# The first layer of the state rows by seven quarter products, set between the products of the last batch

## The chip, the cores and the metric

The kernel runs on one core of a Trainium2 chip. The metric is the device time of one execution in microseconds, as a median of several runs. In what follows TensorE is PE (its weight loads are PEld), VectorE is DVE, ScalarE is ACT, GpSimd is POOL and SyncE, whose queue issues the DMAs, is SP.

## The reference

For each of 8 batches and 8 heads, 512 rows `x` and 32 rows `state` of width 64 attend to each other. The concatenated result is 544 rows of width 512 per batch, and these go through a two-layer network that takes the larger of two linear maps as its hidden layer.

```python
scores = scale * x @ state.T;   a  = softmax(scores);   xread = a @ state     # 512 rows per batch
scores2 = scale * state @ x.T;  a2 = softmax(scores2);  sread = a2 @ x        # 32 state rows per batch
rows = concat([xread, sread])            # (8 * 544, 512)
h1 = rows @ w1; h2 = rows @ w2           # 512 -> 1024
out = maximum(h1, h2) @ w_out            # 1024 -> 512, f32
```

## The kernel before

Since max(h1, h2) = h2 + relu(h1 - h2), the kernel keeps `wd` = w1 - w2 and folds w2 @ w_out into `wwo`. The hidden layer of some rows is then relu(rows @ wd), kept transposed with hidden units on the partitions, and the output is the hidden layer times `wo` plus rows times `wwo`.

The first batches are issued by an order written out by hand (`ORDER`). Batches 2 to 6 go through one loop (`for b in range(2, B - 1)`), which also prepares the attention of batch `n = b + 1`. Batch 7 and the 256 state rows stand in the straight code behind the loop, called the last part here. Every engine works through its own queue in the order in which the code issues.

- `l1_mm`, `l1_ev` (lines 374 and 381): the hidden layer of a batch, eight banks of two 512-column matmuls, and the relu of each bank into `r`, by ACT and DVE in turn.
- `product`, `opened`, `r_sum`, `w_sum`: the second layer. It is a 2 by 2 block product done with seven products in place of eight (Strassen's scheme, in Winograd's form). `r_sum` makes the sums of the left blocks in `st` (part of big5), four per batch on DVE; `w_sum` made those of the weights in `wt`, once, two of them on POOL. One `product` is eight 256-column matmuls. `keep` copies a partial result out of PSUM to `part` (part of big6), `put` adds it to another result into the output tile.
- `m1` (line 472): the hidden layer of the state rows, directly. Eight banks f, each four matmuls of 256 columns (`wd` as weights, `sread_t`, the transposed state rows, moving), and a relu on ACT into `rs_r` (part of w2m).
- `m_product` with `m_sum`: the second layer of the state rows, by the same seven products. `m_sum(k, aq, sst, "P")` sums blocks of `sread_t` into `sst` (xb0) on POOL at the end of the loop, `m_sum(k, bq, rst, "V")` sums blocks of `rs_r` into `rst` (sf0) on DVE.
- `mul` (line 277) is the softmax's scaling on POOL, `difference` and `v_sum` (line 404) are POOL sums of weights.
- `check_sums` (lines 676 to 678): three DVE instructions at the end of b = 6, which look for a softmax sum out of range and leave `bad`. A PE matmul (line 813) adds `bad` over the partitions. It stands in PE's queue ahead of `l1_mm` of batch 7. The general path behind the last branch isn't run here.

The PSUM banks are handed out by `bank("r")`, a ring of five.

Of the kernel before, what the change touches and what calls it, by code (L numbers as in the profile page):

```python
# [10 lines left out]
BF16 = mybir.dt.bfloat16  # L11
ACTF = mybir.ActivationFunctionType
ALU = mybir.AluOpType
# [41 lines left out]
def kernel(  # L55
# [9 lines left out]
    nc = tc.nc  # L65
    B, H, S, D = x.shape
    _, _, Ns, _ = state.shape
# [4 lines left out]
    NF = FF // 128  # L72
# [15 lines left out]
    def bank(ring="r", dtype=F32):  # L88
        if isinstance(ring, int):
            i = ring  # L90
        else:
            r = rings[ring]
            i = r[turn[ring] % len(r)]
            turn[ring] += 1
        return banks[i] if dtype == F32 else banks[i].bitcast(BF16)

    def copy(eng, o, i):
        if eng == "A":
            nc.scalar.copy(o, i)  # L99
        elif eng == "V":  # L100
            nc.vector.tensor_copy(o, i)  # L101
        else:
            nc.gpsimd.tensor_copy(o, i)  # L103
# [8 lines left out]
    wd, = many(1, "wd", [4, FF])  # L112
# [8 lines left out]
    rs_r = w2m[:, 0:NF * NT].rearrange("p (f t) -> p f t", f=NF)  # L121
# [15 lines left out]
    big = many(10, "big", [2048], F32)  # L137
# [11 lines left out]
    wt = big[3].bitcast(BF16).rearrange("p (k f n) -> p k f n", k=4, f=4)  # L149
    st = big[5].bitcast(BF16).rearrange("p (k f t) -> p k f t", k=4, f=4)  # L150
# [214 lines left out]
    def relu(o, p, eng=None):  # L365
        if eng is None:
            flip[0] ^= 1
            eng = "A" if flip[0] else "V"
        if eng == "A":
            nc.scalar.activation(out=o, in_=p, func=ACTF.Relu)  # L370
        else:
            nc.vector.tensor_scalar(o, p, scalar1=0.0, scalar2=None, op0=ALU.max)  # L372
# [8 lines left out]
    def l1_ev(p, b, f, eng=None):  # L381
        relu(r_s[b % 2][:, f, :], p, eng)
# [20 lines left out]
    def add(eng, o, i0, i1, op=ALU.add):  # L403
        (nc.gpsimd if eng == "P" else nc.vector).tensor_tensor(o, i0, i1, op=op)  # L404

    def wq(j, k):
        return wo[:, 4 * j:4 * j + 4, 256 * k:256 * k + 256]

    def rq(b, i, j):
        return r_s[b % 2][:, 4 * j:4 * j + 4, 256 * i:256 * i + 256]  # L410
# [5 lines left out]
    def r_sum(b, k, eng):  # L416
        a, c, op = ((rq(b, 1, 0), rq(b, 1, 1), ALU.add), (st[:, 0], rq(b, 0, 0), ALU.subtract),
                    (rq(b, 0, 0), rq(b, 1, 0), ALU.subtract), (rq(b, 0, 1), st[:, 1], ALU.subtract))[k]
        add(eng, st[:, k], a, c, op)
# [5 lines left out]
    def product(pv, lhs, rhs, first=False, cc=(0, 1)):  # L425
        for c in cc:
            for f in range(4):
                nc.tensor.matmul(pv[c], lhs[:, f, 128 * c:128 * c + 128], rhs[:, f, :],  # L428
                                 start=first and f == 0 and (c == 0 or pv.split), stop=False, skip_group_check=True)
# [18 lines left out]
    def keep(k, pv, eng):  # L448
        if pv.split:
            for c in range(2):  # L450
                copy(eng[c], part[:, k, 256 * c:256 * c + 256], pv[c])
        else:
            copy(eng, part[:, k], pv.p[0])
# [14 lines left out]
    def store(b, c0=0, c1=NC, lo=0, hi=DM, eng=None):  # L468
        dst = out[b * L:b * L + S].rearrange("(p c) n -> p c n", c=NC)
        (eng or nc.sync).dma_start(out=dst[:, c0:c1, lo:hi], in_=ob(b)[:, c0:c1, lo:hi])  # L470

    def m1(f, eng=None):
        p = bank("r")
        for i in range(4):
            nc.tensor.matmul(p[:, 0:NT], wd[:, i, f * 128:(f + 1) * 128], sread_t[:, i, :],  # L475
                             start=(i == 0), stop=(i == 3))
        relu(rs_r[:, f, :], p[:, 0:NT], eng)
# [14 lines left out]
    sst = xb_s[0].rearrange("p c m -> p (c m)")[:, 0:1024].rearrange("p (k f t) -> p k f t", k=4, f=2)  # L492
# [5 lines left out]
    def aq(i, j):  # L498
        return sread_t[:, 2 * j:2 * j + 2, 128 * i:128 * i + 128]
# [4 lines left out]
    def v_sum(k, eng):  # L504
        a, c = ((vq(0, 1), vq(0, 0)), (vq(1, 1), ws[:, 0]), (vq(1, 1), vq(0, 1)), (vq(1, 0), ws[:, 1]))[k]
        add(eng, ws[:, k], a, c, ALU.subtract)
# [6 lines left out]
    def m_product(p, la, lb, ra, rb, first=False):  # L513
        for f in range(2):
            nc.tensor.matmul(p, la[:, f], ra[:, f], start=first and f == 0, stop=False, skip_group_check=True)  # L515
        for f in range(4):
            nc.tensor.matmul(p, lb[:, f], rb[:, f], start=False, stop=False, skip_group_check=True)  # L517

    def m_out(t, k):
        return rs_o[:, t, 256 * k:256 * k + 256]  # L520

# [94 lines left out]
    def sw_range(b, z):  # L616
# [16 lines left out]
        wt=w_sum, rs=r_sum, dif=difference,  # L633
# [13 lines left out]
    for tok in ORDER.split():  # L647
        name, _, at_ = tok.partition("@")
        name, _, eng = name.partition(">")
# [86 lines left out]
    for b in range(2, B - 1):  # L736
        n = b + 1
        if b + 2 < B and b != 3:
            xt_dma(b + 2)
        if b < 4:  # L740
            nc.vector.reciprocal(rr_all[:, b - 2], srd[:, b - 2, 0:130:129])
        for f in range(NF):
            l1_ev(l1_mm(b, f), b, f)
        pX, pY, pZ = Pair(BX), Pair(BY), Pair(BZ)
        pp = [sc_mm(n, hh) for hh in range(2)]
        for hh in range(2):
            sc_ev(pp[hh], n, hh)
        product(pX, rq(b, 0, 0), wq(0, 0), True)
        keep(0, pX, "A")
        r_sum(b, 0, "V")  # L750
        red(n, 0)
        mul(n, 0, "P")
        r_sum(b, 1, "V")
        product(pZ, rq(b, 0, 1), wq(1, 0), True)
        opened(b, pZ, 0, so_half(b, 0))
        pg = [sw_mm(n, 512 * z, 512 * z + 512, BY if z == 0 else "r") for z in range(3)]
        sw_ev(pg[0], n, 0, 512, 0, "A")
        sw_ev(pg[0], n, 0, 512, 1, "A")
        red(n, 1)
        mul(n, 1, "P")  # L760
        at_dma(n)
        if b == 3:
            xt_dma(b + 2)
        if b == 2:
            store(1)
        if b + 4 < B - 1:
            for g in range(2):
                load_x(b + 4, g)
        elif b + 4 < B:
            load_x(b + 4, 0, n=H)  # L770
        r_sum(b, 2, "V")
        product(pX, st[:, 1], wt[:, 1])
        sw_ev(pg[1], n, 512, 1024, 0, "A")
        keep(1, pX, "A")
        put(b, 0, 0, pZ, 0)
        sw_ev(pg[1], n, 512, 1024, 1, "V")
        sw_ev(pg[2], n, 1024, 1536, 0, "A")
        product(pY, st[:, 0], wt[:, 0], True)
        keep(2, pY, "A")
        r_sum(b, 3, "V")  # L780
        sw_ev(pg[2], n, 1024, 1536, 1, "A")
        if b + 2 < B:
            for k in range(4):
                cast_e(b + 2, k, "P")
        difference(n, "P")
        if b + 3 < B:
            for g in range(2):
                cast_b(b + 3, g, "P")
        if b < 6:
            v_sum(b - 2, "P")  # L790
        product(pX, st[:, 2], wt[:, 2])
        opened(b, pX, 1, so_half(b, 1))
        p = sr_mm(n, "r")
        put(b, 1, 1, pX, 2)
        sr_ev(p, n)
        if b < 4:
            srd_ev(b - 2)
        if n == B - 1:
            check_sums()
        product(pY, st[:, 3], wq(1, 1))  # L800
        opened(b, pY, 0, so_half(b, 1))
        put(b, 0, 1, pY, 1)
        product(pX, rq(b, 1, 1), wt[:, 3])
        opened(b, pX, 1, dif[:, b % 2])
        if b < 4:
            sr_cp(sr_tr(b - 2, "r"), b - 2, "A")
        sr_cp(sr_tr(n, "r"), n, "A")
        put(b, 1, 0, pX, None, "A")
        if n == B - 1:
            for k in range(4):  # L810
                m_sum(k, aq, sst, "P")
            p = bank("r")
            nc.tensor.matmul(p[:, 0:1], full, bad, start=True, stop=True)
            nc.vector.tensor_copy(flag[0:1, :], p[0:1, 0:1])
        store(b)


    b = B - 1
    for f in range(NF):
        l1_ev(l1_mm(b, f), b, f)  # L820
    for k in (0, 1, 2, 3):
        r_sum(b, k, "V")
    for f in range(NF):
        m1(f, "A")
    fv = nc.values_load(flag[0:1, 0:1], skip_runtime_bounds_check_because="compared with zero alone")
    pX, pY, pZ = Pair(BX, "r"), Pair(BY), Pair(BZ)
    product(pX, rq(b, 0, 0), wq(0, 0), True)
    keep(0, pX, "AV")
    product(pZ, rq(b, 0, 1), wq(1, 0), True)
    opened(b, pZ, 0, so_half(b, 0))  # L830
    put(b, 0, 0, pZ, 0)
    store(b, 0, 2, 0, 256)
    for k in (0, 1, 2, 3):
        m_sum(k, bq, rst, "V")
    product(pX, st[:, 1], wt[:, 1])
    keep(1, pX, "AV")
    product(pY, st[:, 0], wt[:, 0], True)
    keep(2, pY, "A")
    tc.mark_branch_hint_location("gen", "LikelyTaken", [ENG.PE, ENG.Activation, ENG.DVE, ENG.Pool, ENG.SP])
    mX, mY, mZ = (bank("r")[:, 0:256] for _ in range(3))  # L840
    m_product(mX, aq(0, 0), bq(0, 0), vq(0, 0), wq(0, 0), True)
    copy("A", mk[:, 0], mX)
    m_product(mZ, aq(0, 1), bq(0, 1), vq(1, 0), wq(1, 0), True)
# [63 lines left out]
```

## Time and profile before

| | |
|---|---|
| time, three runs | 143.7, 144.05, 144.55 us; median 144.05 us |
| span of the profiled execution | 141.9 us; its own time isn't listed, and the median lies 2.15 us above the span |
| granted PE clock, mean | 0.995 |
| PE busy / DVE / ACT / POOL | 132.1 / 103.9 / 88.4 / 72.6 us |
| chain that ended last, by engine | PE 85%, DMA 6%, DVE 2%, SP's queue 2% |
| first layer of the state rows, `m1` | 3.49 us on the chain, from 121.93 us |

A row of the timeline has the start, the length from the first start to the last end, the engine, the line, the operation and its tiles, and in brackets the idle time ahead of it with what released it. A row of the chain has start, share of the chain in us, and what. A group has busy time, mean ns of one instruction, and idle time. A PE matmul's length in a row is longer than the step to the next matmul, because matmuls overlap.

### The profile page before, as it was taken

To read this page: it belongs to the slowest core of one execution; us is meant where nothing else is said; L and a number is where in the kernel's file an instruction comes from. 1 tells how busy PE (TensorE), PEld (TensorE's weight loads), DVE (VectorE), ACT (ScalarE), POOL (GpSimd) and SP (SyncE) were. 2 spreads that over 40 slices of the span, in tenths; PEclk is the share of its full clock that TensorE was granted. 3 is DMA by queue.
4 is the path that set the end of the run, shared out by engine and by line. 5 is a ranking of instruction groups with operands and counts; after the bars stand their busy time and mean duration, and the time that the engine had idled before them with its cause. 6 is when DMAs were issued, how large, how long until landed. Compare 5 with 4: busy or idle time off the path is not lost.

```text
span 141.9 us, 3651 instructions
## 1 busy us (share of the span) xinstructions
PE 132.1 (93%) x1432; PEld 93.6 (66%) x1442; DVE 103.9 (73%) x193; ACT 88.4 (62%) x172; POOL 72.6 (51%) x99
## 2 busy tenths in 40 slices
PE   6585999999999999999999999999999999999980
PEld 2264735456787776786778577857876786788860
DVE  3488969778999748984898489569948986848320
ACT  4367968886599547665874769087737745753220
POOL 4147326089109993599179809963980544200000
PEclk9999999999999999999999999999999999999998
DMA  4999999954999999999947999669217041502073
GB/s 120 332 372 389 388 381 388 347 100 78 180 316 288 72 273 259 248 255 270 390 167 137 222 385 161 134 222 225 48 34 296 2 79 69 229 0 79 2 257 120
DMA packets 36452, 29.50 MB, mean 208 GB/s; under 512 B 22608, under 2 KB 32336, under 8 KB 35536
## 3 DMA queue, kind: packets, MB, share of 16 engines
q1 hardware_dynamic: 36160, 29.10, 74.9%
q8 instruction: 12, 0.20, 0.6%
q10 hardware_dynamic: 272, 0.13, 0.3%
q14 instruction: 8, 0.07, 0.1%
HBM read 15.20 MB, written 8.91 MB: 170 GB/s over the span
## 4 chain that ended last, share of the span: by engine, by line
PE 85%; DMA 6%; DVE 2%; SPq 2%; ACT 1%; issue 1%; DVEq 0%
PE bank L428 36%; PE bank L377 18%; PE bank L434 10%; DMA big<-in_moe_w_dram 6%; PE bank L354 5%; PE bank L608 5%; PE bank L475 2%; PE bank L517 2%; PE bank L261 2%; PE bank L301 2%; SPq L164 1%; PE bank L515 1%; DVE w2m L101 1%; DVE r L372 1%; PE bank L550 1%
## 5 line engine op out<-in xcount | busy, mean ns | idle before, releaser
L372 DVE TENSOR_SCALAR r<-bank 128x512 bf16<-128x512 f32 x32 | 21.9, 690 | 13.0 <-PE bank L377 11.9
L277 POOL TENSOR_TENSOR a<-e,er 128x512 bf16<-128x512 bf16 x14 | 17.2, 1235 | 27.4 <-ACT big L99 16.3
L99 ACT COPY big<-bank 128x512 f32<-128x512 f32 (+2 forms) x40 | 21.9, 552 | 12.8 <-PE bank L434 5.5
L377 PE MATMUL bank<-at,sw 128*128 128x512 bf16 x120 | 29.1, 379 | 0.6 <-DVE sw L101 0.2
L428 PEld LDWEIGHTS <-big 128*128 128x128 bf16 x256 | 23.9, 98 | 6.1 <-DVE big L404 2.1
L99 ACT CAST sw<-bank 128x512 bf16<-128x512 f32 x36 | 20.1, 609 | 6.0 <-PE bank L354 6.0
L428 PE MATMUL bank<-big,big 128*128 128x256 bf16 x192 | 23.1, 273 | 0.1
L404 DVE TENSOR_TENSOR big<-bank,big 128x512 f32<-128x512 f32 (+1 forms) x25 | 16.5, 663 | 8.3 <-PE bank L434 7.9
L377 PEld LDWEIGHTS <-sw 128*128 128x128 bf16 x128 | 12.2, 97 | 13.5 <-ACT sw L99 0.5
L370 ACT ACTIVATE r<-bank 128x512 bf16<-128x512 f32 x32 | 18.3, 596 | 4.1 <-PE bank L377 3.9
L428 PEld LDWEIGHTS <-r 128*128 128x128 bf16 x192 | 18.2, 98 | 2.7 <-issue 0.5
L103 POOL CAST xe<-big 128x512 bf16<-128x512 f32 x23 | 15.6, 709 | 6.2 <-DMA big<-in_x_dram 6.2
L103 POOL CAST xb<-big 128x1024 bf16<-128x1024 f32 x12 | 13.1, 1111 | 4.7 <-DMA big<-in_x_dram 4.7
L428 PE MATMUL bank<-wo,r 128*128 128x256 bf16 x128 | 15.5, 273 | 0.0
L434 PE MATMUL bank<-sw,at 128*128 128x256 bf16 x96 | 14.4, 273 | 0.0
L99 ACT COPY sread_t<-bank 128x128 bf16<-128x128 bf16 x8 | 3.2, 472 | 17.3 <-PE bank L338 14.0
L434 PEld LDWEIGHTS <-at 128*128 128x128 bf16 x128 | 12.5, 98 | 1.7
L404 DVE TENSOR_TENSOR big<-r 128x1024 bf16<-128x1024 bf16 x16 | 11.6, 723 | 0.6
L273 DVE TENSOR_REDUCE sums<-e 128x16 f32<-128x512 bf16 x16 | 10.8, 674 | 0.0
L269 ACT ACTIVATE e<-bank 128x512 bf16<-128x512 f32 x16 | 8.9, 596 | 1.9 <-PE bank L261 1.4
L404 POOL TENSOR_TENSOR big<-sw 128x512 bf16<-128x512 bf16 x8 | 9.2, 1150 | 1.3 <-issue 1.3
L101 DVE CAST sw<-bank 128x512 bf16<-128x512 f32 x12 | 7.9, 681 | 1.0 <-PE bank L354 1.0
(100 smaller groups left out, 181.8 us busy)
## 6 DMA issues: line engine op xcount, KB each, us to landing
big<-in_x_dram SPq DMA_DIRECT2D x14, 512.0 KB, 7.8
out_dram<-big SPq DMA_DIRECT2D x7, 1024.0 KB, 6.0
big<-in_moe_w_dram SPq DMA_DIRECT2D x8, 512.0 KB, 11.5
big<-in_moe_w_out_dram SPq DMA_DIRECT2D x4, 512.0 KB, 11.0
big<-in_x_dram SPq DMA_DIRECT2D x1, 1024.0 KB, 6.9
out_dram<-big SPq DMA_DIRECT2D x4, 256.0 KB, 2.7
sf<-in_state_dram SPq DMA_DIRECT2D x1, 384.0 KB, 10.4
out_dram<-w2m SPq DMA_DIRECT2D x2, 128.0 KB, 2.4
```

Of the source, the lines that this page charges most:

```text
L99: nc.scalar.copy(o, i)
L101: nc.vector.tensor_copy(o, i)
L103: nc.gpsimd.tensor_copy(o, i)
L269: nc.scalar.activation(out=e_view(e_s[b % 2], hh).rearrange("p (g c) i n -> p g c (i n)", g=2), in_=p.rearrange("p (c g m) -> p g c m", c= ...
L273: nc.vector.tensor_reduce(es_all[:, b, hh], e_view(e_s[b % 2], hh), axis=AXX, op=ALU.add)
L277: (nc.gpsimd if eng == "P" else nc.vector).tensor_mul(e_view(a_s[b % 2], hh), e_view(e_s[b % 2], hh), er_s[b % 2][:, hh].unsqueeze(3).to_b ...
L370: nc.scalar.activation(out=o, in_=p, func=ACTF.Relu)
L372: nc.vector.tensor_scalar(o, p, scalar1=0.0, scalar2=None, op0=ALU.max)
L377: nc.tensor.matmul(p, sw_s[b % 3][:, g, f * 128:(f + 1) * 128], at_s[b % 3][:, g].rearrange("p c t -> p (c t)"), start=(g == 0), stop=(g = ...
L404: (nc.gpsimd if eng == "P" else nc.vector).tensor_tensor(o, i0, i1, op=op)
L428: nc.tensor.matmul(pv[c], lhs[:, f, 128 * c:128 * c + 128], rhs[:, f, :], start=first and f == 0 and (c == 0 or pv.split), stop=False, ski ...
L434: nc.tensor.matmul(pv[c], at_s[b % 3][:, g, 2 * i + c, :], rhs[:, g, :], start=False, stop=False, skip_group_check=True)
```

## The change

`m1` is no longer called in the last part. The first layer of the state rows becomes a 2 by 2 block product with seven `q_product`s, each of eight 128-column matmuls. The four sums of blocks of `wd` are made by `d_sum` on POOL, two in b = 5 and two in b = 6, and lie in big9 (`wdt`). Three kept results go to big0 (`qk`) by ACT. `q_out` ends a block: on DVE an addition and a relu, or for the last block a relu on ACT. The `q_product`s stand between the first products of batch 7, two of the four `r_sum`s move behind them, and all four `m_sum`s of `rst` stand behind the last `q_product`. The banks of `q_product` are used again by `m_product`.

```diff
+    wdt = big[9].bitcast(BF16).rearrange("p (k f n) -> p k f n", k=4, f=2)
+    qk = big[0][:, 0:1536].rearrange("p (k n) -> p k n", k=3)
+    def dq(j, k):
+        return wd[:, 2 * j:2 * j + 2, 512 * k:512 * k + 512]
+    def d_sum(k, eng):
+        a, c = ((dq(0, 1), dq(0, 0)), (dq(1, 1), wdt[:, 0]), (dq(1, 1), dq(0, 1)), (dq(1, 0), wdt[:, 1]))[k]
+        add(eng, wdt[:, k], a, c, ALU.subtract)
+    def q_product(p, la, rd, first=False):
+        for t in range(4):
+            for f in range(2):
+                nc.tensor.matmul(p[:, 128 * t:128 * t + 128], rd[:, f, 128 * t:128 * t + 128], la[:, f],
+                                 start=first and t == 0 and f == 0, stop=False, skip_group_check=True)
+    def q_out(i, k, p, kept=None):
+        o = rs_r[:, 4 * k:4 * k + 4, 128 * i:128 * i + 128]
+        if kept is None:
+            relu(o, p.rearrange("p (f t) -> p f t", f=4), "A")
+        else:
+            add("V", o, p.rearrange("p (f t) -> p f t", f=4), qk[:, kept].rearrange("p (f t) -> p f t", f=4))
+            nc.vector.tensor_scalar(o, o, scalar1=0.0, scalar2=None, op0=ALU.max)
...
         if b < 6:
             v_sum(b - 2, "P")
+        if b in (5, 6):
+            for k in (0, 1) if b == 5 else (2, 3):
+                d_sum(k, "P")
         product(pX, st[:, 2], wt[:, 2])
...
-    for k in (0, 1, 2, 3):
+    for k in (0, 1):
         r_sum(b, k, "V")
-    for f in range(NF):
-        m1(f, "A")
     fv = nc.values_load(flag[0:1, 0:1], skip_runtime_bounds_check_because="compared with zero alone")
     pX, pY, pZ = Pair(BX, "r"), Pair(BY), Pair(BZ)
+    qX, qY, qZ = (bank("r") for _ in range(3))
+    q_product(qX, aq(0, 0), dq(0, 0), True)
+    copy("A", qk[:, 0], qX)
+    q_product(qZ, aq(0, 1), dq(1, 0), True)
+    q_out(0, 0, qZ, 0)
     product(pX, rq(b, 0, 0), wq(0, 0), True)
     keep(0, pX, "AV")
+    q_product(qY, sst[:, 0], wdt[:, 0], True)
+    copy("A", qk[:, 2], qY)
+    q_product(qX, sst[:, 1], wdt[:, 1])
+    copy("A", qk[:, 1], qX)
     product(pZ, rq(b, 0, 1), wq(1, 0), True)
     opened(b, pZ, 0, so_half(b, 0))
     put(b, 0, 0, pZ, 0)
     store(b, 0, 2, 0, 256)
+    q_product(qX, sst[:, 2], wdt[:, 2])
+    q_out(1, 1, qX, 2)
+    q_product(qY, sst[:, 3], dq(1, 1))
+    q_out(0, 1, qY, 1)
+    for k in (2, 3):
+        r_sum(b, k, "V")
+    product(pX, st[:, 1], wt[:, 1])
+    keep(1, pX, "AV")
+    q_product(qX, aq(1, 1), wdt[:, 3])
+    q_out(1, 0, qX)
+    product(pY, st[:, 0], wt[:, 0], True)
+    keep(2, pY, "A")
     for k in (0, 1, 2, 3):
         m_sum(k, bq, rst, "V")
-    product(pX, st[:, 1], wt[:, 1])
-    keep(1, pX, "AV")
-    product(pY, st[:, 0], wt[:, 0], True)
-    keep(2, pY, "A")
...
-    mX, mY, mZ = (bank("r")[:, 0:256] for _ in range(3))
+    mX, mY, mZ = (q[:, 0:256] for q in (qX, qY, qZ))
```

POOL's queue from the end of b = 5 to the end of b = 6, before. In order: `difference`, `v_sum`, the two `mul`s of batch 7, `difference`, and the first `m_sum` into xb0.

```order
L404 TENSOR_TENSOR big6_115<-sw0_102 128x512
L404 TENSOR_TENSOR sb0_82<-wwo0_76,sb0_82 128x512
L277 TENSOR_TENSOR a1_94<-e1_92,er1_96 128x8x64 x2
L404 TENSOR_TENSOR big6_115<-sw1_103 128x512
L404 TENSOR_TENSOR xb0_89<-sread_t0_78 128x256
```

The two `mul`s follow straight on `v_sum`, and the `m_sum`s straight on `difference`. The same place in the changed kernel, where big9 holds the sums of `wd`:

```order
L404 TENSOR_TENSOR big6_115<-sw0_102 128x512
L404 TENSOR_TENSOR sb0_82<-wwo0_76,sb0_82 128x512
L404 TENSOR_TENSOR big9_118<-wd0_75 128x1024
L404 TENSOR_TENSOR big9_118<-wd0_75,big9_118 128x1024
L277 TENSOR_TENSOR a1_94<-e1_92,er1_96 128x8x64 x2
L404 TENSOR_TENSOR big6_115<-sw1_103 128x512
L404 TENSOR_TENSOR big9_118<-wd0_75 128x1024
L404 TENSOR_TENSOR big9_118<-wd0_75,big9_118 128x1024
L404 TENSOR_TENSOR xb0_89<-sread_t0_78 128x256
```

Two sums of 1024 elements came in ahead of the `mul`s of batch 7, and two behind the last `difference`, ahead of the `m_sum`s.

DVE's queue in the last part, before, from the third `r_sum` (into big5) over the load of the flag, `keep` and `put` to the first two `m_sum`s (into sf0):

```order
L404 TENSOR_TENSOR big5_114<-r1_106 128x1024
L404 TENSOR_TENSOR big5_114<-r1_106,big5_114 128x1024
L825 TENSOR_LOAD flag0_811
L101 COPY big6_115<-bank3_66 128x256
L404 TENSOR_TENSOR big7_116<-bank0_63,big6_115 128x2x256
L404 TENSOR_TENSOR sf0_81<-w2m0_80 128x512
L404 TENSOR_TENSOR sf0_81<-sf0_81,w2m0_80 128x512
```

All four `r_sum`s stand ahead of `keep` here, and the `m_sum`s straight behind `put`. The changed kernel's DVE queue from that `keep` to the same two `m_sum`s; the instructions that write w2m are those of `q_out`:

```order
L101 COPY big6_115<-bank6_69 128x256
L404 TENSOR_TENSOR big7_116<-bank0_63,big6_115 128x2x256
L404 TENSOR_TENSOR w2m0_80<-bank2_65,big0_109 128x4x128
L541 TENSOR_SCALAR w2m0_80<-w2m0_80 128x4x128
L404 TENSOR_TENSOR w2m0_80<-bank5_68,big0_109 128x4x128
L541 TENSOR_SCALAR w2m0_80<-w2m0_80 128x4x128
L404 TENSOR_TENSOR big5_114<-r1_106 128x1024
L404 TENSOR_TENSOR big5_114<-r1_106,big5_114 128x1024
L101 COPY big6_115<-bank6_69 128x256
L404 TENSOR_TENSOR sf0_81<-w2m0_80 128x512
L404 TENSOR_TENSOR sf0_81<-sf0_81,w2m0_80 128x512
```

Between `put` and the first `m_sum` there stand now two blocks of `q_out`, two `r_sum`s and the second `keep`.

## The prediction

> **What bounds the kernel now.** I read the page first, then the chain that ended last, then the timeline of each engine from 104 us on. The page gives PE as the bound:
>
> ```profile
> span 141.9 us, 3651 instructions
> PE 132.1 (93%) x1432; PEld 93.6 (66%) x1442; DVE 103.9 (73%) x193; ACT 88.4 (62%) x172; POOL 72.6 (51%) x99
> ```
>
> The chain in the last 25 us has almost nothing but PE in it:
>
> ```profile
> 118.45 0.00 PE bank L813
> 118.46 0.24 PE bank L377
> ...
> 118.75 3.18 PE bank L377 x14
> 121.93 3.49 PE bank L475 x32
> 125.42 1.75 PE bank L428 x16
> 127.17 0.44 PE bank L434 x4
> ```
>
> So a microsecond taken from PE here is a microsecond of the span, and so is each wait put into PE's queue. `m1` takes 3.49 us for 32 matmuls, 0.109 each; two products take 1.75 us. L813 is the matmul that reads `bad`; it costs nothing today because DVE is done in time.
>
> **PE's own saving.** Removed: 32 matmuls of 256 columns, 3.49 us. Added: seven products of eight 128-column matmuls, 56, each with its own weights. The nearest rows are 128-column transposes, each with its own weights, and the weight loads themselves:
>
> ```profile
> 13.51 1.07 PE L550 MATMUL bank<-ident,wb 128*128 128x128 bf16 x16 [1.35 <-ACT wb L99]
> L475 PEld LDWEIGHTS <-wd 128*128 128x128 bf16 x32 | 3.1, 98 | 0.6
> ```
>
> One such matmul alone reads 0.22 us long (its group's mean is 220 ns), so the 16 step by (1.07 - 0.22) / 15 = 0.057 us, though a load reads 98 ns: loads overlap. 56 x 0.057 = 3.17 us, so 0.32 us are saved. Bounds: half of a 256-column step (0.0545) gives 3.05 us and 0.44 saved; loads that did not overlap give 56 x 0.098 = 5.49 us and 2.0 lost. I take 0.32, by the transposes, which are the same form.
>
> **POOL's four new sums.** These, not the products, decide my forecast. What they run beside:
>
> ```profile
> 104.64 1.15 POOL L404 TENSOR_TENSOR sb<-wwo,sb 128x512 bf16<-128x512 bf16 x1
> 111.28 1.31 POOL L277 TENSOR_TENSOR a<-e,er 128x512 bf16<-128x512 bf16 x1 [5.50 <-ACT big L99]
> 115.38 1.16 POOL L404 TENSOR_TENSOR big<-sw 128x512 bf16<-128x512 bf16 x1 [1.29 <-issue]
> 119.01 0.67 POOL L404 TENSOR_TENSOR xb<-sread_t 128x256 bf16<-128x256 bf16 x1 [2.47 <-ACT sread_t L99]
> 109.51 0.69 DVE L404 TENSOR_TENSOR big<-r 128x1024 bf16<-128x1024 bf16 x1
> 111.07 0.63 DVE L404 TENSOR_TENSOR big<-big,r 128x1024 bf16<-128x1024 bf16 x1
> 112.03 1.53 PEld L428 LDWEIGHTS <-big 128*128 128x128 bf16 x15 [0.42 <-DVE big L404]
> 116.59 0.29 DVE L676 TENSOR_SCALAR wb<-sums 128x272 f32<-128x272 f32 x1
> 116.92 0.44 DVE L677 TENSOR_TENSOR wb<-wb,sums 128x272 f32<-128x272 f32 x1
> 117.40 0.44 DVE L678 TENSOR_REDUCE bad<-wb 128x1 bf16<-128x272 f32 x1
> ```
>
> POOL looks idle (5.50 us, then 2.47 us), and one would hide the sums there. But the trace shows that POOL and DVE hold each other up when both read SBUF. The price of one sum, and four meetings:
>
> ```profile
> 29.75 2.12 POOL L404 TENSOR_TENSOR big<-wo 128x1024 bf16<-128x1024 bf16 x1
> 34.89 1.15 POOL L404 TENSOR_TENSOR big<-sw 128x512 bf16<-128x512 bf16 x1
> 35.48 1.11 DVE L404 TENSOR_TENSOR big<-r 128x1024 bf16<-128x1024 bf16 x1
> 42.55 2.06 POOL L277 TENSOR_TENSOR a<-e,er 128x512 bf16<-128x512 bf16 x2 [6.52 <-DVE er L274]
> 43.70 1.45 DVE L404 TENSOR_TENSOR big<-big,r 128x1024 bf16<-128x1024 bf16 x1
> 44.55 1.07 POOL L103 CAST xe<-big 128x512 bf16<-128x512 f32 x1
> 45.08 1.09 DVE L404 TENSOR_TENSOR big<-r 128x1024 bf16<-128x1024 bf16 x1
> 8.23 0.61 POOL L103 CAST xe<-big 128x512 bf16<-128x512 f32 x1 [1.12 <-DMA big<-in_x_dram]
> 8.50 0.63 DVE L101 CAST xe<-big 128x512 bf16<-128x512 f32 x1
> ```
>
> The DVE sum takes 0.63 to 0.69 us alone. At 35.48 it ends at 36.59, 0.55 after POOL's end at 36.04; at 43.70 it ends at 45.15, 0.54 after POOL's second `mul` at 44.61; at 45.08 at 46.17, 0.55 after the cast at 45.62. DVE waits for the whole POOL instruction and then does its own reading. At 8.50 a cast with one SBUF input does the same: 9.13, 0.29 after POOL's 8.84. Where DVE comes first, POOL waits (the 1.31 us at 111.28, against 1.03 for each `mul` at 42.55). The Trainium skill says the same as a rule (SBUF — State Buffer, Who interferes with whom): the shared port pair is an exclusive lock, taken by a DVE instruction with two SBUF inputs or in a two-port mode, and the later one blocks entirely; reductions never do. By that rule L676 and L677 are both exposed and L678 is not; the meeting of a sum with L676's kind is not in this trace, only the cast's.
>
> End of b = 5. The two sums run from 105.79 (end of the 104.64 row) to 105.79 + 2 x 2.12 + 0.07 for the dependence = 110.10, ahead of the `mul` at 111.28. The DVE sum due at 109.51 waits to 110.10 and ends at 110.65 in place of 110.20, 0.45 late; so the second one (111.07) ends at 112.15, and the weights that PE loads from it at 112.03 come some 0.15 us late: **+0.15**, between 0 and 0.25. `mul` and the transposes' DMA slip by 0.45 too, covered by the stall that follows.
>
> End of b = 6. The third sum follows the `difference` of 115.38; POOL starts its next instruction some 0.04 before the end of the last, so at 116.50, 0.09 us ahead of L676 at 116.59. It holds the port to 118.62. L676 then needs 0.15, to 118.77; the fourth sum has asked since 118.69 and gets the port next, to 120.89. L677, which depends on L676, reads after it, to 121.19; L678 ends at 121.67. PE gets `bad` at 121.73, against 118.45: **+3.28 us**, on the chain, because the whole `l1_mm` of batch 7 is queued behind that matmul. Queued behind L676 on DVE are a `put`, the flag and the relus, none of which PE needs earlier. Bounds: 0 if DVE isn't held, 3.4 if each sum takes a gap more.
>
> The `m_sum`s on POOL move from 119.01 to 121.2, done by 124; the `q_product` that reads the first stands 5 us into PE's delayed work, so they cost nothing. Without the stall they would still be in time by about 1 us.
>
> **DVE in the last part.** Rows that price it:
>
> ```profile
> 122.76 0.69 DVE L404 TENSOR_TENSOR big<-r 128x1024 bf16<-128x1024 bf16 x1
> 123.49 0.69 DVE L404 TENSOR_TENSOR big<-big,r 128x1024 bf16<-128x1024 bf16 x1
> 124.10 0.68 DVE L404 TENSOR_TENSOR big<-r 128x1024 bf16<-128x1024 bf16 x1
> 124.70 0.68 DVE L404 TENSOR_TENSOR big<-r,big 128x1024 bf16<-128x1024 bf16 x1
> 127.70 0.69 DVE L404 TENSOR_TENSOR big<-bank,big 128x512 f32<-128x512 f32 x1 [0.94 <-PE bank L434]
> 128.31 0.42 DVE L404 TENSOR_TENSOR sf<-w2m 128x512 bf16<-128x512 bf16 x1
> 128.76 0.42 DVE L404 TENSOR_TENSOR sf<-sf,w2m 128x512 bf16<-128x512 bf16 x1
> 129.10 0.42 DVE L404 TENSOR_TENSOR sf<-w2m 128x512 bf16<-128x512 bf16 x1
> 130.62 0.42 PEld L517 LDWEIGHTS <-sf 128*128 128x128 bf16 x4
> ```
>
> Steps from start to start: 0.61 for a 0.69 instruction, 0.73 where the next depends on it, 0.45 and 0.34 for `m_sum`. On the clock of before, `put` starts 1.68 us earlier (four `q_product`s of 0.45 ahead of it in place of 3.49), at 126.02. Then come 0.61, twice an addition and a relu (0.73 + 0.21 each), two `r_sum`s (0.61 each), `keep` (0.34), two `m_sum`s (0.45 + 0.42): the second ends at 130.94. The relu over 512 bf16 in SBUF isn't in the trace; its ends are 0.29 (L676, 272 elements) and 0.42 us (`m_sum`, two inputs), less 0.08 to the next start; I take the lower, the same operation. PE wants these sums as weights at 130.62 - 0.32 = 130.30, so it waits 0.64 to 0.9 us: **+0.75**. Today they are ready 1.4 us early.
>
> Hidden: ACT's three copies and one relu, 0.6 us each, replace eight relus over 3.44 us; each is read two products later. The first two `q_product`s need banks whose relus end as PE arrives (0.05 us at most). The flag's load waits behind work already queued. No DMA is added; SP waits only for `put`.
>
> **Sum** on the profiled execution: 141.9 + 0.15 + 3.28 - 0.32 + 0.75 = 145.76 us span, and with the 2.15 us between span and median 147.9 us; the median and the profile differ by that constant alone.
>
> **Rivals.**
> 1. One of the two races goes the other way. If L676 is first (116.59), it ends at 116.88, the third sum at 119.0, L677 waiting since 116.92 at 119.3, L678 at 119.78: PE waits 1.39 us, sum 146.0. If L677 gets in between the two sums, 1.29 us; if only L677 is held, 1.0 us. So 145.6 to 146.0. For it speaks how small the margins are, 0.09 and about 0.1 us; against it, the timeline's order. Chance 0.28.
> 2. The sums don't hold up the check: `bad` is ready before PE asks at 118.39. That needs both L676 and L677 done ahead of the third sum, or a port that gives way for short reads, so the third sum starting after 117.2, or L677 held by less than 0.5 us. Then -0.32 + 0.75: 144.5, not slower by what counts, and 143.7 if DVE keeps up. For it: L676's kind isn't seen blocked here. Against: four meetings, one pattern. Chance 0.13.
> 3. PE comes back slow from a 3.3 us wait. At the kernel's start eight 512-column matmuls step far wider than the 14 of L377 above (3.18 / 14 = 0.227):
>
> ```profile
> 1.29 3.25 PE L577 MATMUL bank<-wz 128*128 128x512 bf16 x8 [1.29 <-DVE ones L580]
> ```
>
> Eight at 0.227 would take 1.8 us, so 1.4 us go: 149.3. The page TensorE: Matmul & The Clock Gate of the Trainium skill (The HAM clock gate) halves the clock after an idle window of about 3.4 us. The granted clock here is 0.995 on the mean, and no PE wait in the trace is nearly as long. Chance 0.05.
>
> **How the numbers follow.** My case, two sums and the check in turn, has 0.50, with 147.2 to 148.4 us as its own range (0.3 on the stall, 0.3 on DVE's backlog); rival 1 has 0.28, rival 2 0.13, rival 3 0.05, and 0.04 is left for loads that don't overlap or a gain I don't see. 147.9 is the first case's time. The range reaches down to rival 1's lower end less 0.3: 145.3 to 148.4. Half a per cent, 0.72 us, is about what a measurement of this kernel tells from no change: slower 0.85 (cases 1, 3 and mine, most of the rest), same 0.13 (rival 2), faster 0.02.
>
> **What will show it.** L700 (today's L676) reads about 2.1 us long from 116.6, L701 about 2.4 us; PE idles some 3.3 us ahead of the matmul that reads `bad`, and the chain goes through DVE and POOL there. The 56 products step by 0.057 us. PE's weight load from sf waits 0.6 to 0.9 us for DVE near the end. I am wrong if L700 to L702 read as today, or if the new sums take far from 2.12 us.

## The result and the profile after

| | before | changed |
|---|---|---|
| time, median | 144.12 us (143.7 to 144.55, 4 runs) | 149.11 us (147.59 to 149.79, 4 runs) |
| ratio, 95% interval | | 1.0335 [1.0298, 1.0373] |
| span of the profiled execution | 141.9 us | 145.8 us (its time: 147.59 us) |

The changed kernel is 3.4% slower. It was forecast slower, but the median lies 1.2 us above the predicted 147.9 us and 0.7 us outside the range. The profiled execution, 147.59 us, is the fastest of the four; the other three took 148.99 to 149.79 us, and the trace of one like those is shown under same_again.

The page of the changed kernel, the chain that ended last by engine:

```profile
PE 78%; DVE 11%; DMA 5%; ACT 2%; issue 1%; SPq 1%; POOL 1%; DVEq 0%
```

PE's share of the chain fell from 85 to 78%, and DVE's rose from 2 to 11%. Where DVE came in is seen in the timeline around the end of b = 6 (start, length, engine, line, operation, and in brackets the idle time with its releaser):

```profile
116.92 2.12 POOL L404 TENSOR_TENSOR big<-wd 128x1024 bf16<-128x1024 bf16 x1
117.07 2.12 DVE L700 TENSOR_SCALAR wb<-sums 128x272 f32<-128x272 f32 x1
118.99 2.18 POOL L404 TENSOR_TENSOR big<-wd,big 128x1024 bf16<-128x1024 bf16 x1
119.23 2.24 DVE L701 TENSOR_TENSOR wb<-wb,sums 128x272 f32<-128x272 f32 x1
121.50 0.44 DVE L702 TENSOR_REDUCE bad<-wb 128x1 bf16<-128x272 f32 x1
122.00 0.16 PE L840 MATMUL bank<-bad,full 128*128 128x1 bf16 x1 [3.07 <-DVE bad L702]
```

L700 reads 2.12 us instead of 0.29 and ends 0.15 us after the third sum (119.19 and 119.04); L701 reads 2.24 instead of 0.44 and ends 0.30 after the fourth (121.47 and 121.17). The reduction is as long as ever. PE waited 3.07 us for `bad`. The chain behind it (start, us, what):

```profile
122.45 3.18 PE bank L377 x14
125.63 0.89 PE bank L532 x16
```

In this execution PE came back at full pace: 14 matmuls of `l1_mm` in 3.18 us, as before. Two `q_product`s take 0.89 us.

### The profile page after: what moved, and what is told of

Read it like the earlier page. It is cut to its first block, busy times and chain, and to the rows that moved or that the text cites. A ratio compares the mean times of both kernels' runs of the same rounds, so it can differ in the third digit from the quotient of the medians.

```text
span 145.8 us, 3708 instructions
## 1 busy us (share of the span) xinstructions
PE 133.3 (91%) x1456; PEld 94.7 (65%) x1466; DVE 110.0 (75%) x199; ACT 87.8 (60%) x168; POOL 81.6 (56%) x103
## 4 chain that ended last, share of the span: by engine, by line
PE 78%; DVE 11%; DMA 5%; ACT 2%; issue 1%; SPq 1%; POOL 1%; DVEq 0%
PE bank L428 31%; PE bank L377 19%; PE bank L434 8%; DMA big<-in_x_dram 5%; PE bank L632 4%; PE bank L354 4%; DVE big L404 3%; PE bank L261 2%; PE bank L517 2%; PE bank L323 2%; DVE wb L701 2%; DVE wb L700 1%; PE bank L574 1%; PE bank L301 1%; PE bank L532 1%
## 5 line engine op out<-in xcount | busy, mean ns | idle before, releaser
L99 ACT COPY big<-bank 128x512 f32<-128x512 f32 (+2 forms) x43 | 23.5, 553 | 14.8 <-PE bank L434 5.5
```

## The experiments

The theory after the result had three parts: the third and fourth sum hold up the check through the port that POOL and DVE share; PE's wait of 3.07 us for `bad` follows from that; and in most executions PE then works at half its clock for a while, which is what the median has above the forecast. Rivals: the excess lies in the new products or in DVE's backlog behind them, or it is no property of the kernel.

**same_again: the changed kernel once more**, with no edit, for a trace of another execution.

> The changed kernel once more, unchanged, for a trace of one of its longer executions (the four so far: 147.6, 149.0, 149.2, 149.8 us, and the trace at hand is of the 147.6 one). Theory 1 (the check waits for GpSimd, and after that wait TensorE restarts at half its pace in most executions): in a longer execution the 16 matmuls of the hidden layer of batch 7 behind the wait take 4.5 to 5.2 us in place of 3.47, and the rest of the trace is as before. Theory 2 (the extra 1.5 us comes from somewhere else, the new products or the loads at the start): those 16 matmuls take 3.5 us, and the time is lost at another place. Median 148.5 to 149.5 us by both.

Measured: 149.77 us (148.96 to 150.4), ratio 1.0392 [1.0332, 1.0452], the traced execution 148.96 us with a span of 147.2 us. Its chain behind the wait, in which `bad` is read at 121.67:

```profile
122.12 4.87 PE bank L377 x14
126.99 0.89 PE bank L532 x16
```

The same 14 matmuls, in the same order, take 4.87 in place of 3.18 us: **+1.69 us**. Behind them both traces agree again (two `q_product`s in 0.89). PE's granted clock, asked for in windows around that place (length, PE busy with its instructions, granted clock, DMA share, GB/s), first of same_again, then of the changed kernel's first trace:

```profile
118.69:122.11 3.42, 0.40 (x2) 1.00 0.00 0
122.11:125.52 3.41, 3.40 (x8) 0.50 0.75 305
```

```profile
117.33:120.75 3.42, 1.60 (x16) 1.00 0.04 9
120.75:124.16 3.41, 2.11 (x10) 1.00 0.26 108
```

The boundaries of these windows aren't chosen freely. The trace records the clock in stretches, and their lengths are multiples of 3.413 us (39 of them between two changes in the first trace, 34 and 6 in this one), so the clock is set on a grid of 3.41 us whose place in the span is another in each execution. In same_again the idle time of PE, 118.61 to 121.67, lies almost all in one window: PE was busy for 0.40 us of it, and the next window runs at 0.50. In the first trace a boundary at 120.75 cuts the idle time in two; PE was busy for 1.60 and 2.11 us in the two windows, and the clock stays at 1.00. The page TensorE: Matmul & The Clock Gate of the Trainium skill (The HAM clock gate) says that the activity window is about 3.4 us and free-running, which these records bear out; that an idle window is needed before the clock drops is stricter than what they show, since 0.40 us of work in the window, and 1.11 us below, did not prevent it.

**fill_wait: work for PE in the wait.** Twelve dummy matmuls ahead of the one that reads `bad`, into the same bank (eleven of them are in the trace).

```diff
             p = bank("r")
+            for _ in range(12):
+                nc.tensor.matmul(p, ident, wd[:, 0, 0:512], start=True, stop=True)
             nc.tensor.matmul(p[:, 0:1], full, bad, start=True, stop=True)
```

> Twelve matmuls of 512 columns (12 x 0.217 = 2.6 us) stand ahead of the matmul that reads the check's result, in the 3.07 us in which TensorE is idle there; the wait itself stays. Theory 1 (half pace after the wait): TensorE is never idle for long, so every execution is like the short one, 147.2 to 147.9 us. Theory 2 (the extra time has another place): no help, 148.5 to 149.5 us.

Measured: 147.88 us (147.46 to 148.75), ratio 1.0255 [1.0189, 1.032]. PE's timeline:

```profile
119.05 2.54 PE L841 MATMUL bank<-wd,ident 128*128 128x512 bf16 x11
122.07 0.16 PE L842 MATMUL bank<-bad,full 128*128 128x1 bf16 x1 [0.48 <-DVE bad L702]
122.10 3.61 PE L377 MATMUL bank<-at,sw 128*128 128x512 bf16 x16
```

The stall is as long as before (`bad` comes at 122.0), only PE has something to do in it, and `l1_mm` keeps full pace. On the same chip that is 1.9 us less than same_again. So the excess over the forecast is the clock after the wait; the wait itself, the products and the backlog were all still there. (The clock is read from the one traced execution, 147.96 us; of the other three only the times are known.)

**sums_alone: the kernel before, with the four sums added** as in the change, and nobody reading them.

```diff
... (wdt, dq and d_sum as in the change)
             v_sum(b - 2, "P")
+        if b in (5, 6):
+            for k in (0, 1) if b == 5 else (2, 3):
+                d_sum(k, "P")
```

> The kernel before, with the four sums of wd added on GpSimd at the places of the changed kernel, and nothing else: their result is not used, and the first layer of the state rows is computed as before. Theory 1: the check waits for the third and fourth sum just the same, 3.3 us, and TensorE restarts slowly in most executions: 147.3 to 149.0 us. Theory 2: 147.4 us in every execution, as the extra time belongs to the products. Rival (the sums cost nothing, the loss is the products'): 144.1 us.

Measured: 149.2 us (148.89 to 150.44), ratio 1.0363 [1.0292, 1.0434]. The timeline, and PE's clock in two windows of the grid (the third and fourth sum start at 116.56 and 118.64):

```profile
116.72 2.12 DVE L686 TENSOR_SCALAR wb<-sums 128x272 f32<-128x272 f32 x1
118.87 2.24 DVE L687 TENSOR_TENSOR wb<-wb,sums 128x272 f32<-128x272 f32 x1
121.64 0.16 PE L826 MATMUL bank<-bad,full 128*128 128x1 bf16 x1 [3.07 <-DVE bad L688]
```

```profile
119.39:122.80 3.41, 1.11 (x6) 1.00 0.00 0
122.80:126.22 3.42, 3.42 (x10) 0.50 0.76 309
```

Four sums on an idle engine, in nobody's way by the program, cost 5.0 us (149.2 less 144.24); the whole change costs 5.5 on the same chip (149.77). Nearly all of the loss is the sums', not the products'.

**sums_early: the sums away from the check.** The first in b = 4, two in b = 5, the fourth on DVE behind the flag.

```diff
-        if b in (5, 6):
-            for k in (0, 1) if b == 5 else (2, 3):
+        if b in (4, 5):
+            for k in (0,) if b == 4 else (1, 2):
                 d_sum(k, "P")
...
             nc.vector.tensor_copy(flag[0:1, :], p[0:1, 0:1])
+            d_sum(3, "V")
```

> The changed kernel with its sums elsewhere: the first in b = 4, two in b = 5 on GpSimd, where it idles, and the fourth on VectorE behind the flag. The check meets no sum. Theory 1: the 3.1 us wait and the slow restart both go; what stays is 0.1 us in b = 6, -0.37 us for the products and 0.6 us for VectorE's backlog: 144.1 to 144.6 us. Theory 2: the wait goes, but 1.5 us stay: 145.6 to 146.2 us.

Measured: 145.28 us (144.72 to 146.22, 10 runs), ratio 1.0066 [1.0031, 1.0101]: most of the loss is gone, but it is 0.7 us above the range I gave. The timeline and the chain of one execution (146.0 us) say why:

```profile
109.04 2.13 POOL L404 TENSOR_TENSOR big<-wd 128x1024 bf16<-128x1024 bf16 x1
110.55 1.17 DVE L404 TENSOR_TENSOR big<-r 128x1024 bf16<-128x1024 bf16 x1
117.81 0.29 DVE L700 TENSOR_SCALAR wb<-sums 128x272 f32<-128x272 f32 x1
120.42 1.89 PE L377 MATMUL bank<-at,sw 128*128 128x512 bf16 x7 [0.76 <-DMA at<-a]
```

```profile
115.64 4.75 DMA at<-a
```

The check (L700) reads 0.29 us again. What is late is `at`. The last transposes of batch 7 were issued at 115.64, against 114.12 before: 1.04 us of this the execution had lost earlier (`l1_mm` of batch 6 starts at 106.10 instead of 105.06), and 0.48 us come from the sum at 109.04, which held up an `r_sum` (1.17 us instead of 0.69) and all that follows it on DVE. Then they took 4.75 us to land, where before took 3.1. PE waits 0.76 us for them.

**no_check: the changed kernel without the check.** The three DVE instructions are left out (`bad` is set to zero), so the sums stand where the change put them but have nothing to hold up there.

```diff
         if n == B - 1:
-            check_sums()
+            nc.vector.memset(bad, 0.0)
```

> The changed kernel with its sums where they are, but the three VectorE instructions of the check are left out (bad is set to zero; the sums' range is not looked at). Theory 1 (the loss is the check's wait for the two sums and what follows from it): TensorE's 3.1 us wait and the slow restart go; what is next is the transposes of batch 7 (at<-a), which in every kernel with these sums landed 4.7 to 4.8 us after issue, not 3.1: a wait of about 0.8 us. 145.0 to 145.6 us. Rival (the products or their banks cost the time): 147 us or more.

Measured: 145.38 us (145.26 to 146.75, 4 runs), ratio 1.0105 [1.0033, 1.0178]. The chain and the timeline:

```profile
114.64 4.75 DMA at<-a
```

```profile
119.44 1.89 PE L377 MATMUL bank<-at,sw 128*128 128x512 bf16 x7 [0.77 <-DMA at<-a]
```

Without the check 1.2 us of the loss are left (145.38 less 144.18, the kernel before on the same chip), of 5.0 us in the result and 5.5 in same_again. In the place of the wait for `bad` comes a shorter one, 0.77 us, for the same slow transposes as in sums_early. In the changed kernel they land at 119.7, inside the wait for `bad`, and so cost nothing.

**sums_placed: the sums where they hold up nobody.** The first two are cut in halves, one half in b = 4 and three in b = 5, so that POOL is done ahead of `r_sum`; the last two stand behind the check, and a copy of `bad` of one element on POOL makes them wait for it.

```diff
... (d_half is d_sum for the half f)
-        if b in (5, 6):
-            for k in (0, 1) if b == 5 else (2, 3):
-                d_sum(k, "P")
+        if b in (4, 5):
+            for k, f in ((0, 0),) if b == 4 else ((0, 1), (1, 0), (1, 1)):
+                d_half(k, f, "P")
...
             check_sums()
+            copy("P", gt, bad)
+            for k in (2, 3):
+                d_sum(k, "P")
```

> The changed kernel with its sums only where no VectorE instruction with two SBUF inputs is due: a half in b = 4, three halves in b = 5 (done by 109.2, ahead of the sum at 109.5), the last two behind the check, by a small copy on GpSimd that waits for it. Theory 1: no wait for the check, the transposes land as before; left are the products (-0.37 us) and VectorE's backlog of 0.6 us, with up to 0.4 us more for the sums beside r_sum: 144.3 to 144.9 us. Rival (the sums still hold up something): 145.3 us or more.

Measured: 144.57 us (144.27 to 145.53, 12 runs), ratio 1.0029 [0.9999, 1.006]. The timeline around the check and in the last part, and two rows of the waits from 118 us on (us in total, times, longest):

```profile
117.33 0.29 DVE L704 TENSOR_SCALAR wb<-sums 128x272 f32<-128x272 f32 x1
118.78 2.13 POOL L404 TENSOR_TENSOR big<-wd 128x1024 bf16<-128x1024 bf16 x1
119.02 0.17 PE L847 MATMUL bank<-bad,full 128*128 128x1 bf16 x1
124.22 1.04 DVE L404 TENSOR_TENSOR big<-big,r 128x1024 bf16<-128x1024 bf16 x1
125.90 0.67 DVE L545 TENSOR_SCALAR w2m<-w2m 128x512 bf16<-128x512 bf16 x1
```

```profile
PEld L517 <- DVE sf L404: 0.9, 1, 0.9
PE bank L517 <- DVE sf L404: 0.6, 1, 0.6
```

At the check the sums now cost nothing: the third runs 1.9 us later, L847 shows no idle time ahead of it, and the transposes land in 3.0 us. What remains is DVE's backlog, a wait of 0.6 to 0.9 us of PE for `m_sum`. It is even longer than in the changed kernel, for POOL's own `m_sum`s come later too and now run beside DVE: an `r_sum` reads 1.04 us instead of 0.69 and the first relu (L545) 0.67 where the other two read 0.29. From `l1_mm`'s first step to PE's last end it is 20.03 us, against 19.64 in the changed kernel and 19.43 before.

**placed_reordered: the backlog taken away as well.** Against sums_placed, `r_sum` 2 and 3 go between the first two and the last two `m_sum`s.

```diff
-    for k in (2, 3):
-        r_sum(b, k, "V")
...
-    for k in (0, 1, 2, 3):
+    for k in (0, 1):
+        m_sum(k, bq, rst, "V")
+    for k in (2, 3):
+        r_sum(b, k, "V")
+    for k in (2, 3):
         m_sum(k, bq, rst, "V")
```

> As sums_placed, and the two late r_sums and the last two m_sums of batch 7 stand behind the first two m_sums in VectorE's queue, so these end 1.2 us earlier. Theory 1 (VectorE's backlog is the rest of the loss): TensorE's weight load from sf no longer waits, 0.5 us less than sums_placed, 143.7 to 144.3 us, which is 0.1 to 0.4 us below the kernel before. Rival: the same time as sums_placed.

Measured: 143.96 us (143.61 to 144.74, 12 runs), ratio 0.9982 [0.9953, 1.001]. It is the best version, and can't be told from the kernel before. Its chain:

```profile
118.57 0.24 PE bank L377
118.86 3.18 PE bank L377 x14
122.05 0.89 PE bank L536 x16
...
123.81 0.94 PE bank L536 x16
...
126.07 0.89 PE bank L536 x16
...
127.83 0.60 PE bank L536 x8
...
137.87 0.37 ACT w2m L99
```

No DVE piece is left. The seven products take 0.89 + 0.94 + 0.89 + 0.60 = 3.32 us on the chain against 3.49 for `m1`, 0.17 less, where 0.32 was told. The part begins 0.11 us later than before (118.57 against 118.46), a delay that this execution already has at 52 us (`l1_mm` at 52.17 against 52.05), long ahead of the change. So only 0.04 us arrives at the end (137.87 against 137.91), but from its first step to PE's last end the part is 0.16 us shorter (19.27 against 19.43). That is what the products themselves are worth by these two traces; the medians can't tell it from nothing.

**writes_alone: POOL writes without reading.** The kernel before, with four fills of 1024 elements on POOL in b = 6 in place of the sums, run once.

```diff
... (wdt as in the change)
+        if b == 6:
+            for k in (0, 1, 2, 3):
+                nc.gpsimd.memset(wdt[:, k], 1.0)
```

> The kernel before with four memsets of 1024 elements on GpSimd in b = 6 at the place of the sums: they write SBUF and read nothing. If what holds VectorE is the shared port's read side, L676's line (one input, two-port mode) may still wait for a memset to end, but L677's (two inputs) reads 0.44 us as alone. If any GpSimd instruction holds VectorE, both are longer. If none, both are as before (0.29 and 0.44 us) and the time is 144 us.

Measured: 148.46 us. The timeline:

```profile
116.28 3.63 POOL L803 MEMSET big<- 128x1024 bf16 x4
116.40 3.67 DVE L686 TENSOR_SCALAR wb<-sums 128x272 f32<-128x272 f32 x1
119.87 0.71 POOL L404 TENSOR_TENSOR xb<-sread_t 128x256 bf16<-128x256 bf16 x1
120.11 0.78 DVE L687 TENSOR_TENSOR wb<-wb,sums 128x272 f32<-128x272 f32 x1
121.42 0.16 PE L826 MATMUL bank<-bad,full 128*128 128x1 bf16 x1 [3.16 <-DVE bad L688]
122.25 4.33 PE L377 MATMUL bank<-at,sw 128*128 128x512 bf16 x14 [0.22 <-issue]
```

L686, with one SBUF input, waits for instructions that only write, and through all four of them; L687, with two SBUF inputs, is held by the `m_sum` that reads. The page SBUF — State Buffer of the Trainium skill (Who interferes with whom) puts a DVE instruction in a two-port mode under the lock against any POOL instruction, and one with two SBUF inputs only against POOL instructions that read; L686 agrees with the first if it runs in such a mode, which no view shows, and of the second this run shows only the half in which POOL reads. PE's wait of 3.16 us is again followed by slow matmuls.

## Why the prediction was right and wrong

**Right: the race at the check.** The four sums read 2.12, 2.12, 2.12 and 2.18 us, priced at 2.12, and the turns came as told: third sum, L700, fourth sum, L701. The first step of `l1_mm` of batch 7 moved from 118.46 to 122.16, 3.70 us. Of these, 0.36 lie far ahead of the change (`l1_mm` at 52.41 against 52.05, and so POOL's first sum at 106.12 where 105.79 was told), 0.12 in the end of b = 5, told +0.15 (the last PE instruction ahead of the check starts at 118.71 against 118.23), and the remaining 3.22 in the check, told +3.28.

**Right in kind: the products.** 16 matmuls step in 0.89 us, 0.0556 each, though one of their weight loads reads 98 ns, so loads overlap as told. 56 at this step would take 3.12 us, so -0.37, told -0.32; where all seven products stand on the chain (placed_reordered) the part gained 0.16.

**Right in kind, a little too dear: DVE's backlog, +0.75.** In the changed kernel's timeline, `put`, the second `m_sum`, and the weight load that waits for it:

```profile
129.70 0.69 DVE L404 TENSOR_TENSOR big<-bank,big 128x512 f32<-128x512 f32 x1 [0.41 <-PE bank L434]
134.14 0.43 DVE L404 TENSOR_TENSOR sf<-sf,w2m 128x512 bf16<-128x512 bf16 x1
134.62 0.33 PEld L517 LDWEIGHTS <-sf 128*128 128x128 bf16 x4 [0.69 <-DVE sf L404]
```

From the start of `put` to the end of that sum it is 4.87 us, told 4.92; the load waits 0.69 us. From `l1_mm`'s first step to PE's last end it is +0.21 us against before, where -0.32 + 0.75 = +0.43 was told: that is 0.37 to 0.58 for the backlog, as the products are taken at -0.16 or -0.37.

**Half right: the transposes' slip, "covered by the stall that follows".** It was covered, but they landed 4.8 us after their issue and not 3.1. Had rival 2 come about, its 143.7 to 144.5 us would have missed this: no_check, in which the check isn't held up, took 145.38.

**The sum.** 145.76 us of span was told for the traced execution and 145.8 came. That it fits so well is luck: 0.36 us of it were lost long ahead of the change, and they make up for 0.09 told too much for the end of b = 5 and the check together (3.34, told 3.43) and 0.22 for the last part (0.21, told 0.43). The 2.15 us added to the span sets a median beside the span of one execution: the traced one took 147.59, 1.79 above its span.

**Wrong: rival 3, given 0.05.** That PE comes back slow from the wait was the case in 7 of 8 executions of this kernel, by their times of 148.96 us or more; the one traced of them (same_again) shows the half clock. The rival's time, 149.3 us, is within 0.2 of the median measured, and its price, 1.4 us from the eight matmuls at the kernel's start, was near the 1.69 measured. What failed is the ground on which it was put aside: "the granted clock here is 0.995 on the mean, and no PE wait in the trace is nearly as long". That PE waits for 1.4 us at most between its matmuls in the trace before is true, but such a trace can't show what a long wait does, and my own case made just such a wait. The rival was no alternative to my case but its sequel. And the 0.995 spoke for the rival: it is a drop to half clock. The two last windows of the trace before (length, PE busy with its instructions, granted clock, DMA share, GB/s), the first of which holds PE's last matmuls:

```profile
137.18:140.59 3.41, 0.70 (x7) 1.00 0.63 204
140.59:141.93 1.34, 0.00 (x0) 0.50 0.00 0
```

These windows lie on the grid of that trace, whose clock record changes at 4.06 and 140.59. Half clock for 1.34 of 141.93 us gives the mean of 0.995, and it came behind a window in which PE was busy for 0.70 us, so 2.71 us of idle time were enough. The profile before showed this, and a stall of 3.28 us was forecast. With the grid of 3.41 us it can be estimated afterwards: half clock needs a window with little PE work in it. At this place the traces show it after 1.11 us of work and not after 1.60, that is with 2.30 us idle and not with 1.81. An idle time of 3.07 us at a chance place on the grid puts at least 2.30 us into one window in 1 - (2 x 2.30 - 3.07) / 3.41 = 55% of the cases, and at least 1.81 us in 84%. So more than half of the chance of my own case belonged at 149.3 us, and the range had to reach to about 149.8.

**Open.** Why the transposes land late is read from traces, not tested. In each of the ten traces the DMA records have one packet of 16,384 bytes of instructions at about that time. Where it begins 2.67 to 2.70 us after the transposes' issue (six traces), they land in 4.7 to 4.8 us, and the last of their 16 completions comes 1.6 us behind the other 15; where it begins 2.45 to 2.49 us after it (four traces), they land in 3.0 to 3.2. The six are also those in which a sum at b = 5 holds up an `r_sum`. Nothing was run that moves the fetch alone.

## What to carry to other kernels

Idle time of POOL is not free to fill: ask of each POOL instruction which DVE instruction falls beside it and who waits for that one, for here four sums that nobody read cost 5 us through two short instructions. A new wait of PE should be priced with its sequel, the matmuls behind it at half clock, unless other matmuls fill it; how short a wait is safe isn't shown here. A mean granted clock below 1.00 says that the clock did drop somewhere: look where, and behind how much idle time, before a long wait is called harmless.

## What was not expected of the hardware

In these traces the clock of PE changes only on a grid of 3.41 us that lies differently in each execution, so that the same wait of 3.07 us costs 1.69 us more or nothing. The first trace of the changed kernel has a half window of its own early in the kernel (columns: length, busy us of PE, PEld, DVE, ACT, POOL with their instructions, granted clock, DMA share, GB/s):

```profile
8.10:11.50 3.40, 3.29 (x31) 2.56 (x32) 2.71 (x6) 1.81 (x3) 2.29 (x3) 0.50 1.03 359
```

The window ahead of it held 1.73 us of PE work by the trace, in 25 instructions, more than the 1.60 us after which the clock stayed up at the check. In sums_early one with 1.98 us was followed by half clock too (from 9.75), in sums_placed one with 1.48 us (from 12.56) was not. So busy time isn't quite what the clock goes by, and the bound between 1.11 and 1.60 us holds for the place of this wait alone. What the early window cost isn't shown: the trace is 0.36 us late at 52 us, but fill_wait and sums_placed, without such a window, are 0.44 and 0.73 us late there.

Four fills on POOL in a row made a DVE instruction of 0.29 us read 3.67 us, while between two sums, the second of which reads the first, DVE got its turn.
